# Two stacked pairs of a memory attention and a hedgehog linear attention on one core: fewer VectorE operations in layer A's features, another chain for layer B's query sums, and a new order

## The chip, the cores and the metric

The kernel runs on 1 core of one Trainium2 chip. The metric is the device time of that core in microseconds (us), from the start to the end of one execution; lower is better.

## The reference, cut to what matters

The input x is 2048 tokens by 512 in bf16. Two kinds of layers, each with 32 heads of 16, are applied twice in the order A, B, A, B, always on the normalized input and with a residual.

```python
# layer A: four segments of 512 tokens, memory M, z carried from one to the next
q, k, v = x @ wq, x @ wk, x @ wv
phi = lambda t: where(t > 0, t + 1.0, exp(t))
for s in range(4):
    a_dot = softmax(qs @ ks.T * 0.25 + causal mask) @ vs
    a_mem = (phi(qs) @ M) / (phi(qs) @ z + 1e-6)
    o = g * a_mem + (1 - g) * a_dot          # g = sigmoid(beta), one per head
    M, z = M + phi(ks).T @ vs, z + phi(ks).sum()
x = x + concat(o) @ wo
# layer B: no mask
pq, pk = q @ w_phi, k @ w_phi
phi_q = [softmax(pq), softmax(-pq)]          # phi_k likewise
kv, z = phi_k.T @ v, phi_k.sum()
x = x + (phi_q @ kv) / (phi_q @ z + 1e-6) @ wo
```

## The kernel before, in words

The kernel holds x in SBUF as 16 tiles of 128 tokens (`X`) and runs the four layers as one program. It is first written down as a list of operations (`Graph.op`), each with its engine, the tiles that it reads and the tiles that it opens. Then a table that is stored in the kernel as a packed text, `ORDER`, says for every operation its place in the one global order, for some of them the engine (an evacuation out of PSUM made by `evac` may go to ScalarE, L359, or to VectorE, L360), and for every tile its buffer. `place` reads the table and `emit` derives the semaphore waits from it. So the order on each engine is that of the table, and an edit that adds or removes an operation comes with a new table.

All of PSUM is four buffers of 128 x 1024 f32 (the pool `D` in the names of the profile). Projections, scores, numerators, sums and transposes each take one of the four. In SBUF the names are those of pools: `p` for general tiles, `pX` for the transposed inputs, `pQ` and `pK` for the masked keys and the queries of layer A, `pV` and `pW` for values, `pF` and `pE` for exponentials, `pT` for weighted values of layer B, `pS` for small sums.

**Normalizing a tile** (`ln`): VectorE makes the statistics (L584, L585); the reciprocal root is an Ln and an Exp on ScalarE (L588, L590) for the four tiles of the first segment and two GpSimd operations (L592, L594) for the others; VectorE normalizes (L605). The result is transposed by DMA or, for the tiles listed in `PE_T`, by TensorE: `tpe` (L379) does eight matmuls with an identity into a PSUM buffer of f32, and an evacuation of 512 columns writes them to bf16.

**Layer A** (`a_proj`, `a_att`): keys, queries and values by matmuls in pairs of row halves (`pair`, L341); the features phi (`phi`, L634) as an exponential on ScalarE (L351) and on VectorE a maximum with 0 (L642), a minimum of the exponential with 1 (L643) and the sum of both (L644); key copies masked by row groups (`kmask`, L651 or L653); scores by matmuls (L326), their exponentials on ScalarE (L351), the products with the values (L326), and on VectorE the reciprocal of the sums, the product (L878) and the addition of the memory's part (L882). `out_proj` multiplies by wo and adds the residual on VectorE (L933).

**Layer B, keys** (`b_keys`, `kv_add`): exponentials of both signs, their sums per head (L980), the values times the reciprocal sums (L1016 straight from PSUM; L1008 from a copy, for pairs listed in `VCOP`), and KV accumulated over all tokens (L946), masked into `Rkv` and `Rz` (L950, L953). Where a residual of layer B is listed in `RES_PE`, the pair of tiles gets X by four matmuls with the identity into its PSUM buffer and ScalarE copies the sum to X (L359).

**Layer B, queries** (`b_query`), four chunks of 512 tokens in each pair of layers. The projection and its two exponentials per group come first. Then 128 small matmuls (L326, from `Rz`) put four sums per head and token into one PSUM buffer `ZQ`: for each sign the softmax's own sum and the sum against z. The weights of both signs are worked out of them by Ln and Exp of -1 on ScalarE (L351, 128 columns each, twice) and by VectorE (L1069 to L1080). Chunk 0 does this from PSUM; chunks 1 to 3 (`ZCOP`) first copy the sums to SBUF and so free the buffer. After that, tile by tile: 16 small matmuls from `Rkv` make the numerators N, a ScalarE copy takes them to SBUF (for tiles in `COPIED`), VectorE multiplies by the weights (L1099 from the copy, L1102 from PSUM), adds both signs (L1105), and transposing and `out_proj` follow. In the first pair of layers the queries and layer A of the second pair run interleaved; in the last pair the queries stand alone at the end, and every two tiles (the last two singly, `SOLO`) are stored when their residual is done.

At the start TensorE does warm-up matmuls on a constant (`warm`, L666) until the first transposed tiles are there.

Of the kernel before, what the change touches and what calls it, by code (L numbers as in the profile page):

```python
# [10 lines left out]
ALU = mybir.AluOpType  # L11
# [286 lines left out]
class Kernel:  # L298
# [72 lines left out]
    def tpe(self, out_ap, src, reads, writes, opens=(), label="", ev=None):  # L371

        ps = self.T(self.pD, "gen")

        def fn(e):
            for k in range(4):
                for hf in range(2):
                    r = slice(64 * hf, 64 * hf + 64)
                    ins = e.matmul(ps.t[:, hf * 512 + k * 64:hf * 512 + k * 64 + 64], src()[r, k * 128:(k + 1) * 128], self.ident[r, r], start=True, stop=True,  # L379
                                   tile_position=(64 * hf, 0))  # L380
            return ins
        self.g.op({"pe": (112.0, fn)}, list(reads) + [self.R("ident")], [ps], opens=opens, label=label + "p", rows=64)
        halves = lambda: ps.t[:].rearrange("p (h x) -> p h x", h=2)[:, :, 0:256].rearrange("p h (a c) -> p h a c", a=4)
        if ev:
            self.evac(ev[0], lambda: ev[1](halves()), 512, [ps], writes, label=label + "e")
        else:
            self.evac(lambda: out_ap().rearrange("p a (h c) -> p h a c", h=2), halves, 512, [ps], writes, label=label + "e")
# [11 lines left out]
    def alloc(self):  # L399
# [10 lines left out]
        self.tri = sb("tri", [128, 64], BF16)  # L410
        self.ones8 = sb("ones8", [128, 8], F32)
# [41 lines left out]
    def setup(self):  # L453
# [66 lines left out]
        for hf in range(2):  # L520
            v(lambda e, hf=hf: e.tensor_copy(self.tri[64 * hf:64 * hf + 64, :], tw.t[64 * hf:64 * hf + 64, 64 * hf:64 * hf + 64]), 100,
              [tw], [R("tri", hf)])
        v(lambda e: e.memset(self.epsln[:], LN_EPS), 70, [], [R("epsln")])
# [57 lines left out]
    def ln(self, t, xT, flex=False, pe=False, root="pool"):  # L581
        R, v = self.R, self.v
        tt = t % 4
        v(lambda e: e.bn_stats(self.stats[:, t, :], self.X[:, t, :]), 602, [R("X", t)], [R("st", t)], label="bn")  # L584
# [29 lines left out]

    def wproj(self, ps, Ws, wres, gs, xT, opens=(), label=""):
# [20 lines left out]
    def phi(self, dst, src, e_, keys, c0, n):  # L636
# [5 lines left out]
        v(lambda e: e.tensor_scalar(cut(dst), cut(src), 0.0, None, op0=ALU.max), 68 + n / 3.84, S, D, label="phmax", port=True)  # L642
        v(lambda e: e.tensor_scalar(cut(e_), cut(e_), 1.0, None, op0=ALU.min), 68 + n / 3.84, E, E, label="phmin", port=True)  # L643
        v(lambda e: e.tensor_tensor(cut(dst), cut(dst), cut(e_), ALU.add), 68 + n / 1.92, D + E, D, label="phadd", port=True)  # L644
# [154 lines left out]
    def a_att(self, L, s, i0):  # L799
# [11 lines left out]
        for gg in range(2):  # L811
            PV = self.T(self.pD, "pv")
            for g in (2 * gg, 2 * gg + 1):
# [5 lines left out]
                for j in range(i0 + 1):  # L819
# [18 lines left out]
                self.mm(lambda S=S, key=key, qry=qry: [  # L838
                    (S.t[:, hf * 512 + p * 192 + 64 * (1 - x):hf * 512 + p * 192 + 192 - 128 * x], key(hf, i0 + 1, p, x), qry(hf, 128 + 64 * x, 128 - 64 * x), p + x == 0, False)
                    for p in range(2) for x in range(2) for hf in range(2)] + [  # L840
                    (S.t[:, hf * 512:hf * 512 + 384].rearrange("p (a b) -> p a b", a=2)[:, :, 0:128], two(hf), tri(hf, 4), False, True) for hf in range(2)],
                    [], rd + trir, [S], opens=[PE], label="Sd", rows=64, dur=286)
                self.act(lambda PE=PE: PE.t[:, :, 64:256], lambda S=S: S.t[:, :].rearrange("p (a b) -> p a b", a=2)[:, :, 0:384].rearrange("p a (c e) -> p a c e", c=2),
                         ACT.Exp, 768, [S], [PE], scale=0.25, label="expd")

# [184 lines left out]
    def b_query(self, L, c, store):  # L1030
# [13 lines left out]
        zv = lambda s, k: ZQ.t[:, :].rearrange("p (a x) -> p a x", a=2)[:, :, 0:256].rearrange("p a (s k x) -> p a s k x", s=2, k=2)[:, :, s, k, :]  # L1044
# [8 lines left out]
        inps = (L, c) not in ZCOP  # L1053
        if not inps:
            ZS = self.T(self.p2, "T")
            two = lambda x: x.rearrange("p (a x) -> p a x", a=2)
            self.evac(lambda: two(ZS.t[:].bitcast(F32)), lambda ZQ=ZQ: two(ZQ.t[:])[:, :, 0:256], 512, zr, [ZS], label="Zev")
            zr = [ZS]
            zv = lambda s, k: two(ZS.t[:].bitcast(F32)).rearrange("p a (s k x) -> p a s k x", s=2, k=2)[:, :, s, k, :]
# [224 lines left out]
```

## Time and profile before

| | before |
|---|---|
| times of 3 runs, us | 468.32, 468.88, 470.64 (median 468.88) |
| profiled execution: its own time | 468.75 |
| its span in the trace | 466.7 |
| mean granted TensorE clock | 0.992 |
| busy: PE (TensorE) | 446.3 |
| busy: ACT (ScalarE) | 423.3 |
| busy: DVE (VectorE) | 420.2 |
| busy: POOL (GpSimd) | 56.2 |

The times are those of the whole execution on the device; the span runs from the first to the last instruction in the trace of one profiled execution. Busy time is the time in which at least one instruction of the engine ran. Matmuls overlap, so a busy TensorE need not be at its peak. In rows of groups the columns are line, engine, operation, output and input with shapes, count, then busy time and the mean in ns of one, then the idle time ahead of them and what ended it. In rows of the timeline they are the start, the length, and then the instructions. In rows of stretches of the span they are the bounds and the length, the busy times of PE, PEld (weight loads), DVE, ACT and POOL with the number of instructions, the granted clock, the DMA share and GB/s.

### The profile page before, as it was taken

To read this page: it belongs to the slowest core of one execution; us is meant where nothing else is said; L and a number is where in the kernel's file an instruction comes from. 1 tells how busy PE (TensorE), PEld (TensorE's weight loads), DVE (VectorE), ACT (ScalarE), POOL (GpSimd) and SP (SyncE) were. 2 spreads that over 40 slices of the span, in tenths; PEclk is the share of its full clock that TensorE was granted. 3 is DMA by queue.
4 is the path that set the end of the run, shared out by engine and by line. 5 is a ranking of instruction groups with operands and counts; after the bars stand their busy time and mean duration, and the time that the engine had idled before them with its cause. 6 is when DMAs were issued, how large, how long until landed. Compare 5 with 4: busy or idle time off the path is not lost.

```text
span 466.7 us, 25467 instructions
## 1 busy us (share of the span) xinstructions
PE 446.3 (96%) x11789; PEld 298.7 (64%) x11789; DVE 420.2 (90%) x800; ACT 423.3 (91%) x552; POOL 56.2 (12%) x138
## 2 busy tenths in 40 slices
PE   8999999999999999998999999999999999999987
PEld 4557756666666776665556776666677677666553
DVE  5999999798799978989999999999997897998985
ACT  3899999999999997689999999999999999677892
POOL 1411123001101101100331022020110020110000
PEclk9999999999999999999999999999999999999799
DMA  8943363631254131100254435344133214200255
GB/s 247 229 107 85 49 82 57 93 55 25 50 75 63 29 47 27 31 3 14 37 83 58 61 73 82 60 70 62 25 50 62 38 26 51 36 13 3 55 86 171
DMA packets 87756, 29.97 MB, mean 64 GB/s; under 512 B 74322, under 2 KB 87650, under 8 KB 87650
## 3 DMA queue, kind: packets, MB, share of 16 engines
q1 hardware_dynamic: 86818, 27.81, 34.4%
q8 instruction: 92, 1.51, 1.4%
q10 hardware_dynamic: 800, 0.52, 0.4%
q14 instruction: 14, 0.11, 0.1%
q0 software_dynamic: 32, 0.02, 0.0%
HBM read 6.31 MB, written 2.10 MB: 18 GB/s over the span
## 4 chain that ended last, share of the span: by engine, by line
PE 57%; ACT 34%; DVE 4%; DMA 3%; issue 2%; POOL 1%; SPq 0%; DVEq 0%
PE D L341 36%; PE D L326 18%; ACT p L351 18%; ACT pF L351 9%; ACT pE L351 4%; DMA p<-p 2%; PE D L666 2%; DMA pX<-p 1%; ACT pS L351 1%; DVE X L933 1%; ACT p L359 1%; DVE p L795 1%; DVE pK L360 0%; POOL rstd L594 0%; ACT X L359 0%
## 5 line engine op out<-in xcount | busy, mean ns | idle before, releaser
L351 ACT ACTIVATE p<-D 128x1024 bf16<-128x1024 f32 (+1 forms) x224 | 221.0, 1027 | 14.5 <-PE D L341 10.2
L326 PE MATMUL D<-pK,pQ 64*128 64x256 bf16 (+3 forms) x1536 | 114.2, 243 | 5.1 <-ACT p L351 1.3
L351 ACT ACTIVATE pF<-D 128x896 bf16<-128x896 f32 x128 | 116.5, 940 | 1.5 <-PE D L326 1.0
L326 PEld LDWEIGHTS D<-pK,pQ 64*128 64x128 bf16 x1536 | 55.4, 94 | 41.5 <-ACT pF L351 5.6
L326 PE MATMUL D<-pV,pF 64*128 64x34 bf16 x1024 | 76.4, 175 | 1.4 <-ACT pF L351 0.8
L326 PE MATMUL D<-pW,pF 64*128 64x34 bf16 x1024 | 73.3, 175 | 0.0
L326 PEld LDWEIGHTS D<-pV,pF 64*128 64x128 bf16 x1024 | 57.0, 93 | 4.1 <-ACT pF L351 1.7
L592 POOL TENSOR_SCALAR rstd<-mv 128x1 f32<-128x1 f32 x60 | 16.2, 275 | 351.8 <-DVE mv L585 351.7
L326 PE MATMUL D<-pV,p 64*128 64x34 bf16 x1024 | 53.9, 176 | 0.2 <-DVE MS L755 0.2
L351 ACT ACTIVATE pE<-D 128x768 bf16<-128x768 f32 x64 | 52.1, 823 | 2.1 <-PE D L326 1.9
L326 PEld LDWEIGHTS D<-pW,pF 64*128 64x128 bf16 x1024 | 52.9, 93 | 0.9
L326 PE MATMUL D<-pW,p 64*128 64x34 bf16 x1024 | 52.7, 176 | 0.0
L326 PEld LDWEIGHTS D<-pV,p 64*128 64x128 bf16 x1024 | 47.9, 93 | 3.4 <-DVE MS L755 0.4
L326 PEld LDWEIGHTS D<-pW,p 64*128 64x128 bf16 x1024 | 46.4, 93 | 2.2
L326 PE MATMUL D<-tri,two 64*128 64x128 bf16 (+1 forms) x384 | 46.7, 234 | 0.0
L584 DVE BATCH_NORM_STATS2 stats<-X 128x6 f32<-128x512 bf16 x64 | 42.6, 681 | 3.8 <-DMA X<-in_A_x_dram 3.6
L326 PE MATMUL D<-pV,pE 64*128 64x34 bf16 x512 | 45.3, 175 | 0.5 <-issue 0.5
L326 PE MATMUL D<-pW,pE 64*128 64x34 bf16 x512 | 42.9, 175 | 0.0
L980 DVE TENSOR_REDUCE pS<-p 128x64 f32<-128x1024 bf16 (+1 forms) x36 | 38.6, 1090 | 0.3 <-ACT p L351 0.2
L594 POOL TENSOR_TENSOR rstd<-rstd,mhalf 128x1 f32<-128x1 f32 x60 | 37.9, 639 | 2.4
L933 DVE TENSOR_TENSOR X<-X,D 128x1024 bf16<-128x1024 bf16 (+1 forms) x30 | 32.1, 1074 | 6.4 <-PE D L341 6.2
L341 PE MATMUL D<-pX,WA_q 64*128 64x512 bf16 x256 | 37.1, 376 | 0.5 <-issue 0.4
(133 smaller groups left out, 998.5 us busy)
## 6 DMA issues: line engine op xcount, KB each, us to landing
pW<-pV SPq DMA_DIRECT2D x16, 136.0 KB, 2.8
out_dram<-X SPq DMA_DIRECT2D x7, 256.0 KB, 2.3
X<-in_A_x_dram SPq DMA_DIRECT2D x3, 512.0 KB, 7.5
pX<-in_B_wqkv_dram SPq DMA_DIRECT2D x3, 512.0 KB, 4.6
p<-p SPq DMA_TRANSPOSE x73, 3.1
pX<-p SPq DMA_TRANSPOSE x54, 3.2
WA_k<-in_A_wk_dram SPq DMA_DIRECT2D x2, 256.0 KB, 6.5
WA_v<-in_A_wv_dram SPq DMA_DIRECT2D x1, 512.0 KB, 7.1
```

What stands on the lines that cost most here:

```text
L326: ins = e.matmul(out_ap, lhsT, rhs, start=st, stop=sp, tile_position=(basep(lhsT), basep(out_ap)))
L341: ins = e.matmul(out_ap, lhsT[64 * hf:64 * hf + 64], rhs[64 * hf:64 * hf + 64], start=k == 0 and i == 0, stop=k == 1 and i == len(lists[hf ...
L351: return self.g.op({"act": (dur, lambda e: e.activation(out_ap(), in_ap(), func, scale=scale))}, reads, writes, opens, label=label)
L359: ch = {"act": (n / 1.2 + 51, lambda e: e.activation(out_ap(), in_ap(), ACT.Copy)), "dve": ((340 if fast else n / 0.96 + 65), lambda e: e. ...
L584: v(lambda e: e.bn_stats(self.stats[:, t, :], self.X[:, t, :]), 602, [R("X", t)], [R("st", t)], label="bn")
L592: v(lambda e: e.tensor_scalar(rs, self.mv[:, t, 1:2], LN_EPS, None, op0=ALU.add), 170, [R("mv", t)], [R("rstd", t)], eng="pool", label="rstd")
L594: v(lambda e: e.tensor_tensor(rs, rs, self.mhalf[:], ALU.pow), 540, [R("rstd", t), R("mhalf")], [R("rstd", t)], eng="pool", label="rstd")
L666: ins = e.matmul(D.t[c0:, r0 * 8:r0 * 8 + n], r[:, c0:], ones(r, n), start=True, stop=True, tile_position=(r0, c0))
L795: v(lambda e: e.tensor_tensor(tmp.t[:].rearrange("p (y h r d) -> p y h r d", y=16, h=2, r=2), NM.t[:, :].rearrange("p (h y r d) -> p y h r ...
L933: self.v(lambda e: e.tensor_tensor(X(), X(), src(), ALU.add), 65 + 512 * n / 0.96, pr + xr, xr, label="res")
L980: fn = lambda e, sgn=sgn, eo=eo, Z=Z, n=n: e.tensor_reduce(Z.t[:, 0:64 * n].rearrange("p (k s h) -> p k s h", k=n, s=2)[:, :, sgn, :], eo( ...
```

## The change

It has seven parts.

1. **phi** in two VectorE operations: max(x, 0) + 1 in one, then the minimum of that and the exponential; the operation L643 is dropped.
2. **`tpe`** writes its transposes as bf16 into PSUM (`is_transpose`), and its evacuation reads bf16.
3. **Query sums**: Ln and Exp of -1 over both signs in one call of 256 columns, straight from PSUM in all chunks; one product (L1085) makes the ratios of both signs, a second operation (L1086) adds them with 1e-6, then Ln and Exp of 128 columns and one product (L1090). The copies of the sums (`ZCOP`) are gone.
4. **The first segment's tile 3** (`LN_ACT`) is normalized with statistics made on ScalarE by accumulating activations (`ln_act`); only its last operation stays on VectorE.
5. **Residuals**: `RES_PE` is empty, so all are added on VectorE (L958 after the change); the 24 identity matmuls and six ScalarE copies are gone.
6. **Copies**: all numerators go through ScalarE's copy (`COPIED`), and one value pair of each last key stage is copied first (`VCOP`). A mask `keep` is made once; the branch that would use it (`TRI_E`) is empty.
7. **`ORDER`** is new.

```diff
 def tpe
-  ins = e.matmul(ps.t[:, hf * 512 + k * 64:hf * 512 + k * 64 + 64], ..., start=True, stop=True, ...)
+  ins = e.matmul(pb()[:, hf * 1024 + k * 64:hf * 1024 + k * 64 + 64], ..., start=True, stop=True, is_transpose=True, ...)
...
 def ln_act
+  a(680, lambda e: e.activation(xn.t[:], self.X[:, t, :], ACT.Copy, accum_out=st(0)), ...)
+  a(100, lambda e: e.activation(st(1), st(0), ACT.Copy, scale=-1.0 / D), ...)
+  a(780, lambda e: e.activation(xn.t[:], self.X[:, t, :], ACT.Square, bias=st(1), accum_out=st(2)), ...)
+  a(185, lambda e: e.activation(st(3), st(2), ACT.Ln, scale=1.0 / D, bias=self.epsln[:, 0:1]), ...)
+  a(100, lambda e: e.activation(st(3), st(3), ACT.Exp, scale=-0.5), ...)
+  self.v(lambda e: e.tensor_scalar(xn.t[:], self.X[:, t, :], st(1), st(3), op0=ALU.add, op1=ALU.mult), 300, ...)
...
 def phi
-  v(lambda e: e.tensor_scalar(cut(dst), cut(src), 0.0, None, op0=ALU.max), ...)
-  v(lambda e: e.tensor_scalar(cut(e_), cut(e_), 1.0, None, op0=ALU.min), ...)
-  v(lambda e: e.tensor_tensor(cut(dst), cut(dst), cut(e_), ALU.add), ...)
+  v(lambda e: e.tensor_scalar(cut(dst), cut(src), 0.0, 1.0, op0=ALU.max, op1=ALU.add), ...)
+  v(lambda e: e.tensor_tensor(cut(dst), cut(dst), cut(e_), ALU.min), ...)
...
 def b_query
-  if not inps:
-      self.evac(lambda: two(ZS.t[:].bitcast(F32)), lambda ZQ=ZQ: two(ZQ.t[:])[:, :, 0:256], 512, zr, [ZS], label="Zev")
...
-  self.act(lambda: u(0), lambda: zv(1, 1), ACT.Ln, 128, zr, [t1[0]], psum=inps, label="zln")
-  self.act(lambda: u(0), lambda: u(0), ACT.Exp, 128, [t1[0]], [t1[0]], scale=-1.0, psum=False, label="zln")
-  v(lambda e: e.tensor_tensor(u(0), u(0), zv(0, 1), ALU.mult), ...)
...
+  self.act(wide, lambda: zv(1), ACT.Ln, 256, zr, [t1], label="zlA")
+  self.act(lambda: t1.t[:], lambda: t1.t[:], ACT.Exp, 256, [t1], [t1], scale=-1.0, psum=False, label="zlA")
+  v(lambda e: e.tensor_tensor(y(), wide(), zv(0), ALU.mult), ...)
+  v(lambda e: e.scalar_tensor_tensor(ys(1), ys(0), 1e-6, ys(1), op0=ALU.add, op1=ALU.add), ...)
+  self.act(lambda: ys(1), lambda: ys(1), ACT.Ln, 128, [AB[1]], [AB[1]], psum=False, label="zlB")
+  self.act(lambda: ys(1), lambda: ys(1), ACT.Exp, 128, [AB[1]], [AB[1]], scale=-1.0, psum=False, label="zlB")
+  v(lambda e: e.tensor_tensor(..., split(t1.t[:]), ys(1)..., ALU.mult), ...)
...
-ZCOP = {(L, c) for L in range(2) for c in (1, 2, 3)}
-VCOP = set()
+TRI_E = set()
+LN_ACT = 3
+VCOP = {(0, 3), (1, 3)}
...
-RES_PE = {(0, t) for t in (2, 3, 6, 7)} | {(1, t) for t in (2, 3, 6, 7, 8, 9, 10, 11)}
+RES_PE = set()
```

Lines shift: L351, L359, L360, L341 and L326 stay where they are, the others move by 1 to 25 (L605 becomes L610, L878 becomes L903, L933 becomes L958, L1016 becomes L1041, L1099 becomes L1111, L1105 becomes L1117, L666 becomes L686, L379 becomes L380).

What moves is shown at three places. The first is the start of the program. On ScalarE before, from its first computation to the first evacuation of a transposed tile (`rstd` is a tile's reciprocal root, `gt` the gate of layer A, `D` a PSUM buffer):

```order
L588 ACTIVATE rstd<-mv,epsln 128x1 x2
L590 ACTIVATE rstd<-rstd 128x1
L588 ACTIVATE rstd<-mv,epsln 128x1
L590 ACTIVATE rstd<-rstd 128x1 x2
L588 ACTIVATE rstd<-mv,epsln 128x1
L351 ACTIVATE gt<-D 128x32
L590 ACTIVATE rstd<-rstd 128x1
L359 ACTIVATE pX<-D 128x2x4x64 x3
```

After, at the same place:

```order
L626 ACTIVATE p,stats<-X 128x512
L627 ACTIVATE stats<-stats 128x1
L628 ACTIVATE p,stats<-X,stats 128x512
L593 ACTIVATE rstd<-mv,epsln 128x1
L629 ACTIVATE stats<-stats,epsln 128x1
L595 ACTIVATE rstd<-rstd 128x1
L593 ACTIVATE rstd<-mv,epsln 128x1
L630 ACTIVATE stats<-stats 128x1
L593 ACTIVATE rstd<-mv,epsln 128x1
L595 ACTIVATE rstd<-rstd 128x1
L351 ACTIVATE gt<-D 128x32
L595 ACTIVATE rstd<-rstd 128x1
```

Tile 3's two passes of 512 columns stand ahead of all roots now, its root stands among them, and the gate's exponential still stands ahead of the last root. On TensorE before, from the gate's matmul on (`onesb` marks the warm-up, `ident` the transposes of the normalized tiles; buffers are numbered here):

```order
L326 MATMUL D1<-beta_sb,onesb 128x32
L666 MATMUL D0<-onesb 128x512 x4
L379 MATMUL D2<-ident,p11 128x64 x8
L666 MATMUL D0<-onesb 128x512 x2
L379 MATMUL D3<-ident,p12 128x64 x8
```

After, at the same place:

```order
L326 MATMUL D1<-beta_sb,onesb 128x32
L686 MATMUL D0<-onesb 128x512 x8
L380 MATMUL D2<-ident,p12 128x64 x8
L686 MATMUL D0<-onesb 128x512 x2
L380 MATMUL D3<-ident,p11 128x64 x8
```

Eight warm-up matmuls instead of four stand between the gate's matmul and the first transposes. The second place is the queries of the last pair of layers. On TensorE before, from the last projections ahead of the first query sums (`pX,WB_q` is a query projection, `Rz` the sums, `Rkv` the numerators):

```order
L341 MATMUL D<-pX,WB_q 128x512 x16
L326 MATMUL D<-Rz,p 128x2x4 x112
L326 MATMUL D<-Rkv,p 128x64 x16
L326 MATMUL D<-Rz,p 128x2x4 x16
L326 MATMUL D<-Rkv,p 128x64 x32
L326 MATMUL D<-Rz,p 128x2x4 x32
L326 MATMUL D<-Rkv,p 128x64 x16
L326 MATMUL D<-Rz,p 128x2x4 x32
L326 MATMUL D<-Rkv,p 128x64 x32
L341 MATMUL D<-pX,WB_q 128x512 x16
```

After, at the same place:

```order
L341 MATMUL D<-pX,WB_q 128x512 x8
L326 MATMUL D<-Rz,p 128x2x4 x112
L326 MATMUL D<-Rkv,p 128x64 x16
L326 MATMUL D<-Rz,p 128x2x4 x16
L341 MATMUL D<-pX,WB_q 128x512 x8
L326 MATMUL D<-Rkv,p 128x64 x32
L326 MATMUL D<-Rz,p 128x2x4 x48
L326 MATMUL D<-Rkv,p 128x64 x16
L326 MATMUL D<-Rz,p 128x2x4 x16
L341 MATMUL D<-pX,WB_q 128x512 x8
L326 MATMUL D<-Rkv,p 128x64 x48
```

Two groups of query projections stand between the small matmuls now, where before all of them stood ahead of or behind them. The third place is VectorE beside this, from the last mask of `Rkv` on; before:

```order
L950 TENSOR_TENSOR Rkv<-KV,H 128x512 x2
L1069 TENSOR_TENSOR pS<-pS,D 128x128
L1071 TENSOR_TENSOR pS<-pS,D 128x128
L1072 TENSOR_TENSOR pS<-pS,D 128x128
L1073 SCALAR_TENSOR_TENSOR pS<-D,pS 128x128
L360 COPY p<-D 128x512
L1080 TENSOR_TENSOR pS<-pS 128x8x16
L1102 TENSOR_TENSOR p<-D,pS 128x1024
L1105 TENSOR_TENSOR p<-p 128x512
```

After:

```order
L975 TENSOR_TENSOR Rkv<-KV,H 128x512 x2
L1085 TENSOR_TENSOR pS<-pS,D 128x2x2x64
L1086 SCALAR_TENSOR_TENSOR pS<-pS 128x128
L1090 TENSOR_TENSOR pS<-pS 128x4x4x16
L1085 TENSOR_TENSOR pS<-pS,D 128x2x2x64
L1111 TENSOR_TENSOR p<-p,pS 128x1024
L1086 SCALAR_TENSOR_TENSOR pS<-pS 128x128
L1117 TENSOR_TENSOR p<-p 128x512
```

The second chunk's sums were copied out (L360) ahead of the first chunk's weights; now its first product (L1085) reads PSUM, between the first chunk's weights and its first product with N.

More of the change, by code (lines that the diff above doesn't have):

```diff
@@ L373, in tpe @@
         ps = self.T(self.pD, "gen")
+        pb = lambda: ps.t[:, :].bitcast(BF16)
         def fn(e):
@@ L583, in ln @@
         tt = t % 4
+        if root == "all":
+            return self.ln_act(t, xT)
         v(lambda e: e.bn_stats(self.stats[:, t, :], self.X[:, t, :]), 602, [R("X", t)], [R("st", t)], label="bn")
@@ L1122, in lnA @@
             for t in range(s * 4, s * 4 + 4):
-                self.ln(t, self.xA[(L, s)], pe=("xA", L, t) in PE_T, root="act" if L == 0 and s == 0 else "pool")
+                self.ln(t, self.xA[(L, s)], pe=("xA", L, t) in PE_T, root=("all" if t == LN_ACT else "act") if L == 0 and s == 0 else "pool")
         for L in range(2):
```

193 lines of the change are left out of this document (100 added, 93 removed).

## The prediction

> **What bounds the kernel now.** I read the page's first parts first: busy time by engine, the granted clock by slices, and the shares of the chain that ended last.
>
> ```profile
> PE 446.3 (96%) x11789; PEld 298.7 (64%) x11789; DVE 420.2 (90%) x800; ACT 423.3 (91%) x552; POOL 56.2 (12%) x138
> PEclk9999999999999999999999999999999999999799
> PE 57%; ACT 34%; DVE 4%; DMA 3%; issue 2%; POOL 1%; SPq 0%; DVEq 0%
> ```
>
> Three engines are nearly full, and two of them, TensorE and ScalarE, make 91% of the chain. VectorE is as busy as ScalarE but ends a wait for only 4% of the span (18.7 us). So an instruction taken from VectorE is worth little by itself, and one taken from ScalarE or TensorE is worth something only in the stage that this engine bounds. I therefore cut the span where the work changes: layer A of the first pair, the start of the first layer B queries, the middle, the last key stage, and the last queries.
>
> ```profile
> 24.00:180.00 156.00, 150.32 (x4434) 105.24 (x4428) 141.94 (x261) 153.10 (x187) 17.59 (x41) 1.00 0.38 62
> 206.00:216.00 10.00, 8.42 (x322) 5.78 (x320) 7.81 (x19) 9.48 (x16) 0.00 (x0) 1.00 0.01 3
> 216.00:394.00 178.00, 173.10 (x4800) 118.08 (x4796) 165.04 (x312) 174.47 (x217) 25.58 (x56) 1.00 0.36 55
> 394.00:428.00 34.00, 33.94 (x680) 22.52 (x676) 31.49 (x52) 25.29 (x37) 3.07 (x8) 1.00 0.14 22
> 428.00:466.70 38.70, 32.23 (x792) 19.30 (x792) 29.83 (x59) 27.54 (x44) 0.00 (x0) 0.90 0.43 94
> ```
>
> The columns are length, then busy time on PE, weight loads, VectorE, ScalarE, GpSimd, then the clock. ScalarE bounds 24 to 180 (153.10 of 156) and 206 to 394 (174.47 of 178 in the second part), with TensorE close behind (173.10 of 178). From 394 to 428 TensorE alone bounds (33.94 of 34, ScalarE 25.29). From 428 on nobody is full and the mean clock is 0.90: here the time goes into chains.
>
> The sum is made against the profiled execution: span 466.7 us in a run of 468.75, so 2.05 us lie around the span. The median of the runs shown, 468.88, is 0.13 above that run.
>
> **ScalarE and TensorE work that goes or comes.**
>
> ```profile
> L341 PE MATMUL D<-X,ident 64*128 64x512 bf16 x24 | 4.6, 378 | 0.2 <-ACT X L359 0.2
> L359 ACT ACTIVATE X<-D 128x1024 bf16<-128x1024 f32 x6 | 6.2, 1036 | 4.4 <-PE D L341 4.4
> L359 ACT ACTIVATE p<-D 128x512 f32<-128x512 f32 x3 | 1.8, 599 | 0.0
> L351 ACT ACTIVATE pS<-pS 128x128 f32<-128x128 f32 x28 | 9.0, 322 | 4.4 <-DVE pS L980 3.8 <-DVE pS L1073 0.4
> L351 ACT ACTIVATE p<-D 128x1024 bf16<-128x1024 f32 x216 | 216.3, 1043 | 12.1 <-PE D L341 7.8 <-PE D L326 3.5
> L933 DVE TENSOR_TENSOR X<-X,D 128x1024 bf16<-128x1024 bf16 x22 | 26.8, 1217 | 5.2 <-PE D L341 4.9
> ```
>
> Six residual pairs lose four identity matmuls each. ScalarE loses six copies into X, three copies of query sums, and gains four copies of N (L1099's source) at 1.04. Its Ln and Exp on query sums become 256 wide in two of four calls per chunk; no row shows that width, so it lies between 322 ns (128) and 1043 ns (1024). By a straight line, 0.80 ns an element, it is 0.42 us: 16 calls by 0.1 are 1.6 us, half in each pair of layers.
>
> Between 206 and 394, where ScalarE bounds, two residual copies (2.1) and one sum copy (0.6) go and 0.8 comes: 1.9 us; overlap of neighbours eats little of it. **Term 1: -1.9.** The ends are 0, if TensorE, 4.9 us short of full there, keeps the stretch, and -5.4, if ScalarE's 3.5 us of idle closes too. The eight identity matmuls of this stage lie under ScalarE's exponentials and count nothing; without that cover they are 8 x 0.19 = 1.5 us at most.
>
> From 428 on ScalarE loses four residual copies (4.1) and two sum copies (1.2), gains four N copies (4.2) and 0.8 of width, and one exponential of the queries (1.0) stands ahead of the first sums now: -1.3. TensorE loses 16 identity matmuls, 3.1 us by the row's busy share. The chain there passes from ScalarE to TensorE, so I take ScalarE's sum, the nearer one. **Term 2: -1.3**, ends +1.0 and -3.1.
>
> At the very end the residuals were shared between two engines:
>
> ```profile
> 462.54 1.02 ACT L359 ACTIVATE X<-D 128x1024 bf16<-128x1024 f32 x1 [4.42 <-PE D L341]
> 463.66 0.69 DVE L933 TENSOR_TENSOR X<-X,D 128x512 bf16<-128x512 bf16 x1 [0.97 <-PE D L341]
> ```
>
> Now VectorE does both in series. The last matmuls of the pair would end near 462.5, the sum takes 1.22, and the last tile's 0.69 follows: 464.4 at the earliest in place of 464.35, more if VectorE comes late from the tiles ahead, whose pairs take 1.22 against 1.74 us of matmuls. **Term 3: +0.4**, ends 0 and +1.5.
>
> **VectorE.**
>
> ```profile
> L643 DVE TENSOR_SCALAR p<-p 128x1024 bf16<-128x1024 bf16 x22 | 9.1, 413 | 0.0
> L360 DVE CAST p<-D 128x512 bf16<-128x512 f32 x11 | 7.5, 679 | 1.5 <-PE D L901 1.5
> L651 DVE TENSOR_SCALAR pQ<-p,m 128x512 bf16<-128x512 bf16 x15 | 4.7, 341 | 0.3 <-ACT p L359 0.3
> L360 DVE COPY p<-D 128x512 f32<-128x512 f32 x3 | 2.1, 692 | 1.0 <-PE D L326 0.9
> L1075 DVE SCALAR_TENSOR_TENSOR pS<-p 128x128 f32<-128x128 f32 x6 | 1.7, 283 | 0.0
> L757 DVE TENSOR_TENSOR MSb<-MS,GAm 128x272 bf16<-128x272 f32 x12 | 5.1, 428 | 0.0
> L1102 DVE TENSOR_TENSOR p<-D,pS 128x1024 bf16<-128x1024 f32 x4 | 4.9, 1221 | 0.1
> L1099 DVE TENSOR_TENSOR p<-p,pS 128x1024 bf16<-128x1024 bf16 x28 | 18.7, 685 | 2.0 <-ACT p L351 1.7
> L1016 DVE TENSOR_TENSOR pT<-D,pT 128x1024 bf16<-128x1024 f32 x28 | 33.0, 1213 | 1.0 <-PE D L341 0.9
> L1008 DVE TENSOR_TENSOR pT<-p,pT 128x512 bf16<-128x512 bf16 x8 | 2.9, 396 | 0.0
> ```
>
> The minimum of layer A's features (22 x 0.413 and four halves) saves 10.2. Ten copies of 512 out of f32 PSUM become six out of bf16 PSUM; that copy has no row and lies between 0.341 (all bf16, in SBUF) and 0.679 (f32 PSUM). I take 0.45, nearer the first because the type is the same: 6.8 becomes 2.7. Three sum copies go (2.1). Forty operations of 0.28 on query sums become eight of 0.28 and 16 of twice the width at 0.43: -2.1. Four N products leave PSUM (4 x 0.54 = 2.1). The two value pairs at the ends of the key stages become one more copy of 1.22 and eight products of 0.396 for four of 1.213: -0.5. Against this stand six residual pairs, 7.3. With the tile that ScalarE normalizes (0.9) the sum is -14.7 of 420.2, or -13.4 with the slow copy. It lies beside exponentials and matmuls; scaled to the 18.7 us of VectorE on the chain it is 14.7 / 420.2 x 18.7. **Term 4: -0.6**, ends 0 and -6.4, all the ScalarE idle of the two long stretches (2.9 and 3.5), for VectorE is the engine that hands ScalarE its PSUM buffers and operands.
>
> **The first tile.**
>
> ```profile
> 7.89 0.61 PE L666 MATMUL D<-onesb 64*128 64x512 bf16 x4
> 8.32 0.30 PE L379 MATMUL D<-ident,p 64*128 64x64 bf16 x8
> 8.67 1.67 ACT L359 ACTIVATE pX<-D 128x512 bf16<-128x512 f32 x3 [0.28 <-PE D L379]
> 10.66 0.37 PE L341 MATMUL D<-pX,WA_k 64*128 64x512 bf16 x1 [0.31 <-ACT pX L359]
> ```
>
> The first projection waits for three evacuations on ScalarE, and those for the first transposes. VectorE saves one tile's statistics (0.85), but the gate's exponential, which waits for TensorE, still stands ahead of the last root on ScalarE. Ahead of the first transposes stand eight warm-up matmuls in place of four, 0.43 us more. **Term 5: +0.4**, ends -0.4 (the statistics count after all) and +0.8.
>
> **The clock.** In these rows TensorE's clock falls, in the queries of the last pair:
>
> ```profile
> 429.00:430.00 1.00, 0.86 (x66) 0.77 (x62) 1.00 (x2) 0.95 (x2) 0.00 (x0) 1.00 0.00 0
> 432.00:433.00 1.00, 0.63 (x26) 0.47 (x20) 0.97 (x3) 0.53 (x2) 0.00 (x0) 0.50 0.00 0
> 438.00:439.00 1.00, 0.93 (x10) 0.34 (x10) 1.00 (x3) 0.82 (x5) 0.00 (x0) 0.76 0.33 71
> 428.91 0.95 PE L326 MATMUL D<-Rz,p 64*128 64x8 bf16 x64
> 436.26 3.10 PE L341 MATMUL D<-pX,WB_q 64*128 64x512 bf16 x16
> 210.85 1.02 PE L341 MATMUL D<-pX,WB_q 64*128 64x512 bf16 x8
> 215.40 1.04 PE L341 MATMUL D<-pX,WB_q 64*128 64x512 bf16 x8
> ```
>
> From 428.91 to 436.26 only matmuls of 8 and 64 columns run; three microseconds into that the clock is 0.50. At the same point of the first pair the query projections stand between the small ones, never over 3.7 us apart, and the clock stays 1.00. The change's order puts such projections between the small ones here too. I take it that the drop goes: the sixteen projections at 436.26 take 3.10 instead of two times about 0.9, and the small ones of this time a little over half a microsecond more than their like at 216. **Term 6: -1.9**, ends 0 (drop stays) and -3.0. [...]
>
> Sum: -1.9 - 1.3 + 0.4 - 0.6 + 0.4 - 1.9 = -4.9, and 468.75 - 4.9 = 463.9 us.
>
> **Rivals.**
>
> *Cover.* In 206 to 394 TensorE takes over when ScalarE gets lighter, VectorE's relief stays under it, and the clock falls again, since sums still wait for a chain of four ScalarE operations with nothing wide behind. Then terms 1, 4 and 6 vanish: 468.75 - 1.3 + 0.8 = 468.2. For it speak the 4.9 us by which TensorE is short of full; against it the projections' new place.
>
> *The held buffer, slower.* All of PSUM is four buffers. Before, chunks 1 to 3 copied their sums out (0.60 or 0.69) and freed the buffer. Now the buffer is held through Ln, Exp and the first product, 0.42 + 0.42 + 0.43, and through whatever each engine does between, one ScalarE copy of 1.04 and one VectorE product of 0.685: 3.0, or 2.3 longer, six times, 13.8 us. If half of it reaches TensorE, whose next matmuls need that buffer, and terms 1 and 6 fail with it, the time is 468.75 - 1.5 + 6.9 = 474. It decides when the wait for a query-sum buffer goes beyond about 0.8 us a chunk (4.9 over six). Against it: in the first chunk, which never copied, TensorE was 8.42 of 10 busy, and the buffer held there cost under 1.6.
>
> *Relief counts.* VectorE's 14.7 us let ScalarE's idle close in both stretches: term 4 is -6.4 and the time 458.
>
> [...]
>
> **How the numbers follow.** This kernel's measurement tells about 0.5% (2.3 us) from no change, so faster means under 466.5 and slower over 471.2. My sum, 461 to 466.4, has 0.44; transposes 0.04 (465.8); relief 0.14 (455.5 to 461); cover 0.25 (466.5 to 471); the held buffer 0.13 (471.3 to 477). Faster is 0.44 + 0.04 + 0.14 = 0.62, same 0.25, slower 0.13. The range leaves out the held buffer and the lower part of relief: 456.5 to 471.
>
> **What would show it.** Right: no slice under 1.00 after 420; ScalarE still full from 24 to 180; VectorE near 406 busy, its bf16 PSUM copies near 0.45; the first projection near 11.1; the last key stage unchanged in length; under 0.5 us of waits of TensorE for the query sums' products. Wrong: a stretch of 0.50 in the last queries (term 6), TensorE idle before query sums until VectorE's first product (the held buffer), a last residual that starts over 1 us after the last matmul (term 3), or long waits for VectorE in 394 to 428.

## The result, and the profile after

The changed kernel takes 472.37 us (median of 22 runs, 469.67 to 475.68) against 469.63 us for the kernel before (22 runs, 468.32 to 471.05): ratio 1.006, 95% interval 1.0043 to 1.0076. It is slower by 0.6%; I had forecast 463.9. The profiled execution after took 472.04 us with a span of 470.0; before it was 468.75 and 466.7.

The page's first parts after the change: busy time by engine, the granted clock, the shares of the chain.

```profile
PE 443.2 (94%) x11765; PEld 295.0 (63%) x11765; DVE 410.4 (87%) x761; ACT 426.9 (91%) x556; POOL 56.0 (12%) x139
PEclk9989999999999999999999999999999999999999
PE 61%; ACT 22%; DVE 13%; issue 2%; DMA 1%; POOL 1%; DVEq 0%
```

The clock is full after 420, as forecast, but a slice near 29 us is below, and VectorE has 13% of the chain in place of 4%. The stages of the prediction, after the change:

```profile
24.00:180.00 156.00, 145.81 (x4258) 101.74 (x4256) 133.62 (x239) 147.43 (x180) 17.44 (x40) 0.99 0.33 55
216.00:394.00 178.00, 171.53 (x4798) 115.49 (x4794) 162.21 (x297) 174.69 (x218) 25.36 (x56) 1.00 0.35 54
428.00:470.00 42.00, 34.12 (x872) 20.67 (x868) 35.01 (x65) 31.36 (x47) 0.00 (x0) 0.99 0.39 87
```

From 24 to 180 ScalarE has 147.43 where it had 153.10: nearly six microseconds of its idle time are new, in the stretch for which I had expected it to stay full.

Fixed times mix stages once one is late, so I compare one event: the masking of KV (`Rkv`), which ends layer B's keys in each pair of layers. Before:

```profile
206.41 1.28 DVE L950 TENSOR_TENSOR Rkv<-KV,H 128x512 bf16<-128x512 f32 x2
428.76 1.29 DVE L950 TENSOR_TENSOR Rkv<-KV,H 128x512 bf16<-128x512 f32 x2
```

After:

```profile
212.64 1.28 DVE L975 TENSOR_TENSOR Rkv<-KV,H 128x512 bf16<-128x512 f32 x2
434.62 1.28 DVE L975 TENSOR_TENSOR Rkv<-KV,H 128x512 bf16<-128x512 f32 x2
```

Up to the first mask the change loses 6.23 us, between the masks it gains 0.37, and from the second to the end of the span (37.94 before, 35.38 after) 2.6. The whole loss lies ahead of the first mask. TensorE's timeline after the change shows its place:

```profile
24.48 0.38 PE L326 MATMUL D<-pK,pQ 64*128 64x256 bf16 x4
29.39 1.89 PE L341 MATMUL D<-pX,WA_k 64*128 64x512 bf16 x8 [4.54 <-DMA pX<-p]
31.05 0.66 PE L326 MATMUL D<-pK,pQ 64*128 64x256 bf16 x4
31.48 1.54 PE L341 MATMUL D<-pX,WA_k 64*128 64x512 bf16 x8
32.85 0.39 PE L326 MATMUL D<-pK,pQ 64*128 64x256 bf16 x4
33.06 1.04 PE L341 MATMUL D<-pX,WA_q 64*128 64x512 bf16 x8
```

TensorE stands 4.54 us before the second segment's first projection, for a DMA, and the next eight matmuls take 1.89 where eight of the same shape take 1.04 at 33.06. The granted clock in stretches of 2 us there:

```profile
26.00:28.00 2.00, 0.00 (x0) 0.00 (x0) 1.52 (x8) 0.83 (x1) 1.29 (x4) 1.00 0.81 150
28.00:30.00 2.00, 0.61 (x4) 0.34 (x6) 0.00 (x0) 0.00 (x0) 1.19 (x3) 0.77 0.74 158
30.00:32.00 2.00, 2.00 (x15) 0.90 (x12) 0.00 (x0) 0.25 (x1) 0.00 (x0) 0.50 0.66 135
```

So the stall is paid twice, as idle time and as half clock behind it. The DMA is a transpose of the normalized second segment. SP's queue, from which it is issued, before and after:

```profile
14.78 1.29 SPq L364 DMA_TRANSPOSE pX<-p  x1
16.12 0.57 SPq L460 DMA_DIRECT2D pX<-in_B_wqkv_dram  x1
16.73 5.04 SPq L364 DMA_TRANSPOSE pX<-p  x3
```

```profile
15.26 0.59 SPq L462 DMA_DIRECT2D pX<-in_B_wqkv_dram  x1
15.89 1.15 SPq L462 DMA_DIRECT2D WA_o<-in_A_wo_dram  x2
17.09 0.43 SPq L462 DMA_DIRECT2D pX<-in_B_wqkv_dram  x1
17.56 3.03 SPq L364 DMA_TRANSPOSE pX<-p  x1
20.64 0.58 SPq L462 DMA_DIRECT2D WB_o<-in_B_wo_dram  x1
21.27 6.42 SPq L364 DMA_TRANSPOSE pX<-p  x3
```

The new order issues all three 512 KB loads of layer B's projections, all of layer A's output weights and seven of the eight 64 KB loads of layer B's output weights ahead of the first transpose. What the four transposes then take from issue to landing (minimum, median, maximum), before and after:

```profile
DMA to landing us min/median/max: 2.7/4.0/5.6
```

```profile
DMA to landing us min/median/max: 2.7/6.4/10.0
```

The last is issued at 26.4 in place of 20.2, though VectorE has normalized the last of the four tiles by 20.44, against 19.89 before. The last of the three 512 KB loads lands at 26.89, and the transposes behind it at 27.57 to 29.15. The first transpose, issued at 17.56 behind all three, lands 10.0 us later, 0.68 us behind the last of them.

### The profile page after: what moved, and what is told of

It reads as the page before. It is cut to its first block, busy times and chain, and to the rows that moved or that the text cites. A ratio compares the mean times of both kernels' runs of the same rounds, so it can differ in the third digit from the quotient of the medians.

```text
span 470.0 us, 25380 instructions
## 1 busy us (share of the span) xinstructions
PE 443.2 (94%) x11765; PEld 295.0 (63%) x11765; DVE 410.4 (87%) x761; ACT 426.9 (91%) x556; POOL 56.0 (12%) x139
## 4 chain that ended last, share of the span: by engine, by line
PE 61%; ACT 22%; DVE 13%; issue 2%; DMA 1%; POOL 1%; DVEq 0%
PE D L341 37%; PE D L326 22%; ACT p L351 11%; ACT pF L351 6%; ACT pE L351 3%; DVE p L1111 2%; PE D L686 2%; DVE X L958 2%; DVE stats L589 2%; DVE pQ L671 1%; DVE p L610 1%; ACT pS L351 1%; DMA p<-p 1%; DVE p L1117 1%; DVE pV L360 1%
## 5 line engine op out<-in xcount | busy, mean ns | idle before, releaser
L351 ACT ACTIVATE p<-D 128x1024 bf16<-128x1024 f32 (+1 forms) x228 | 226.1, 1023 | 16.3 <-PE D L341 8.0
L326 PE MATMUL D<-pK,pQ 64*128 64x256 bf16 (+3 forms) x1536 | 115.1, 244 | 5.1 <-ACT pE L351 0.9
L351 ACT ACTIVATE pF<-D 128x896 bf16<-128x896 f32 x128 | 116.1, 936 | 1.9 <-PE D L326 1.3
L326 PEld LDWEIGHTS D<-pK,pQ 64*128 64x128 bf16 x1536 | 54.7, 94 | 43.1 <-ACT pF L351 5.7
L326 PE MATMUL D<-pV,pF 64*128 64x34 bf16 x1024 | 76.0, 176 | 0.5 <-ACT pE L351 0.2
L326 PE MATMUL D<-pW,pF 64*128 64x34 bf16 x1024 | 73.5, 176 | 0.0
L326 PEld LDWEIGHTS D<-pV,pF 64*128 64x128 bf16 x1024 | 56.7, 93 | 4.2 <-issue 1.3
L351 ACT ACTIVATE pE<-D 128x768 bf16<-128x768 f32 x64 | 52.7, 828 | 2.4 <-PE D L326 2.0
L326 PEld LDWEIGHTS D<-pW,pF 64*128 64x128 bf16 x1024 | 53.4, 93 | 1.3
L326 PE MATMUL D<-pV,p 64*128 64x34 bf16 x1024 | 53.2, 176 | 0.1
L326 PE MATMUL D<-pW,p 64*128 64x34 bf16 x1024 | 52.1, 176 | 0.6 <-issue 0.6
L326 PEld LDWEIGHTS D<-pV,p 64*128 64x128 bf16 x1024 | 47.4, 93 | 3.7 <-issue 1.1
L326 PEld LDWEIGHTS D<-pW,p 64*128 64x128 bf16 x1024 | 46.1, 93 | 2.6 <-issue 0.8
L326 PE MATMUL D<-tri,two 64*128 64x128 bf16 (+1 forms) x384 | 46.3, 234 | 0.0
L326 PE MATMUL D<-pV,pE 64*128 64x34 bf16 x512 | 45.1, 175 | 0.0
L341 PE MATMUL D<-pX,WA_k 64*128 64x512 bf16 x256 | 38.7, 389 | 5.4 <-DMA pX<-p 4.5
L958 DVE TENSOR_TENSOR X<-X,D 128x1024 bf16<-128x1024 bf16 (+1 forms) x36 | 39.3, 1097 | 4.7 <-PE D L341 4.3
L326 PE MATMUL D<-pW,pE 64*128 64x34 bf16 x512 | 43.1, 175 | 0.0
L341 PE MATMUL D<-pX,WA_q 64*128 64x512 bf16 x256 | 37.1, 377 | 0.7 <-DVE p L610 0.6
```

Of the source, the lines that this page charges most:

```text
L326: ins = e.matmul(out_ap, lhsT, rhs, start=st, stop=sp, tile_position=(basep(lhsT), basep(out_ap)))
L341: ins = e.matmul(out_ap, lhsT[64 * hf:64 * hf + 64], rhs[64 * hf:64 * hf + 64], start=k == 0 and i == 0, stop=k == 1 and i == len(lists[hf ...
L351: return self.g.op({"act": (dur, lambda e: e.activation(out_ap(), in_ap(), func, scale=scale))}, reads, writes, opens, label=label)
L958: self.v(lambda e: e.tensor_tensor(X(), X(), src(), ALU.add), 65 + 512 * n / 0.96, pr + xr, xr, label="res")
```

## The experiments

Theory: SP's queue is the cause of the loss, and what I had summed is right beside it. Rivals: the tiles are normalized late, or later parts of the change cost as well. The first four kernels move loads and nothing else; the list of loads is that of `setup`, 15, 16 and 18 the 512 KB ones of layer B, 19 to 26 its output weights, 10 to 13 layer A's output weights, a quarter each (e4 moves all four, e6 and e10 two of them). Each ratio is to the kernel before as it ran beside the experiment on the same chip: 471.87 us for e1 to e4, 470.9 for e6 to e9, 470.67 for e10 and e11, 471.22 for e12 and e13.

**e1**, in `place`, on the changed kernel (`foldT` are the transposes of layer B's weights, `xnT` those of the inputs, `otr` those of the attention outputs, `vsw` the swaps of the values' halves):

```diff
+loads = [o for o in self.ops if o.label == "load"]
+late, last = [loads[i] for i in (15, 16, 18)], [loads[i] for i in range(19, 27)]
+order = [o for o in order if o not in late + last]
+at = lambda label, k: order.index([o for o in order if o.label == label and o.kind == "d"][k])
+k = at("foldT", 7) + 1
+order[k:k] = last
+k = at("xnT", 3) + 1
+order[k:k] = late
```

> The kernel after with eleven weight loads of layer B (three of 512 KB, eight of 64 KB) moved behind the four transposes of the second segment in SP's queue; nothing else changes. Theory (queue): the 4.54 us of idle of TensorE at 24.86 and the 3.41 us at half clock behind it (1.7 us lost) go; 472.4 - 6.2 = 466.2 us, and the last masked KV of the first pair comes 5 to 7 us earlier than in the kernel after. Rival (late operands): the transposes are late because VectorE and GpSimd normalize these tiles later; then the gap stays and the time is 471 to 473. Rival (later buffers): the head is only a part, and the time comes back to 469 to 470.

Measured: 478.28 us, ratio 1.0145 (1.0115 to 1.0176). Slower still. The two waits of TensorE for DMAs from 20 to 70:

```profile
PE D L349 <- DMA p<-p: 6.7, 1, 6.7
PE D L334 <- DMA pW<-pV: 1.5, 1, 1.5
```

The wait for the inputs is gone, so the transposes were not late for their tiles; but the moved loads stand in front of other transfers now, the value swaps (1.5) and the transposes for layer A (6.7, with 10.24 us at half clock from 58.88 on). The first mask comes at 217.41, later than with the change. My expected time was wrong, since I had looked only at what the loads stood in front of and not at what they would stand in front of.

**e2** moves only the output weights, **e3** only the three large loads, by the same lines with one of the two lists empty.

> The kernel after with only the eight 64 KB loads of layer B's output weights moved behind. They are 0.5 MB, eight of the eleven issues, about 0.6 us of SP each. Theory of bytes in the queue: at some 300 GB/s they are worth 1.7 us of the last landing, so the gap of 4.54 shrinks to about 2.9 and the time is 469.5 to 471. Rival (issuing time): eight issues of 0.6 are 4.8 us of SP ahead of the transposes, so the gap goes nearly whole and the time is 466 to 467.5.

Measured: 474.81 us, ratio 1.0057 (1.0038 to 1.0075).

> The kernel after with only the three 512 KB loads of layer B's projection weights moved behind. They are 1.5 MB in three issues, 1.6 us of SP. Theory of bytes: 5 us of the last landing, so the gap of 4.54 goes and the time is 466 to 467.5. Rival (issuing time): 1.6 us of the gap go, and the time is 470 to 471.

Measured: 474.58 us, ratio 1.0052 (1.0027 to 1.0078). In e2 TensorE still waits 3.1 us for the inputs, near the 2.9 of bytes in the queue (that is at 300 GB/s; in the change's profile the DMAs move 283 on average from 8 to 24); in e3 not at all. So bytes count there and issuing time little. Both times come from new waits as in e1 (2.7 us for `p<-p` in e2; 2.3 and 2.3 for `pW<-pV` and `p<-p` in e3) and tell nothing more; the first masks, at 215.05 and 214.31, are later than with the change too.

**e4** is the converse, on the kernel before:

```diff
+early = [loads[i] for i in (15, 18, 10, 11, 12, 13, 19, 20, 21, 22, 23, 24, 25, 26)]
+order = [o for o in order if o not in early]
+k = order.index([o for o in order if o.label == "xnT" and o.kind == "d"][0])
+order[k:k] = early
```

> The kernel before, with two of the 512 KB loads, the eight 64 KB loads of layer B's output weights and four halves of layer A's output weights put ahead of the first transpose of the second segment (a third 512 KB load cannot move, since its buffer is still in use). Theory (queue): the fourth transpose lands 2 to 4 us later than 23.4, TensorE stands idle before the second segment's first projection by 1 to 3 us, and the time rises by 1 to 4 us over the kernel before (471 to 474). Rivals by which the order of loads is harmless: within 1 us of the kernel before.

Measured: 478.05 us, ratio 1.0133 (1.0097 to 1.0169), more than the 1 to 4 us that I had expected. The old kernel stalls at the new one's place, and its first mask of KV comes at 214.74, 8.33 late:

```profile
PE D L346 <- DMA pX<-p: 4.9, 1, 4.9
```

The way there is another one. The loads moved ahead keep SP issuing until 22.6, and the transposes, issued then, land 2.5 us after their issue, where the change's took up to 10.0:

```profile
16.48 6.12 SPq L465 DMA_DIRECT2D WB_o<-in_B_wo_dram  x8
22.65 5.23 SPq L369 DMA_TRANSPOSE pX<-p  x4
```

```profile
DMA to landing us min/median/max: 2.5/2.5/2.6
```

So here SP's issuing time counts, and in e2 and e3 the bytes. Either way the order of loads alone is enough for more than the change lost.

**e6** spreads the loads of the changed kernel by need:

```diff
+wbo, late, wao = loads[19:27], [loads[16], loads[15]], [loads[11], loads[12]]
+order = [o for o in order if o not in wbo + late + wao]
+for k, o in enumerate(wbo):
+    order.insert(900 + 40 * k, o)
+k = at("foldT", 5) + 1
+order[k:k] = wao
+k = at("vsw", 1) + 1
+order[k:k] = late
```

> The kernel after with the loads spread by need: one 512 KB load ahead of the second segment's transposes, the other two behind the value swaps that follow them, half of layer A's output weights behind the sixth transpose of weights, the eight 64 KB loads of layer B's output weights one by one far later (about 90 us on). Theory (queue): the transposes land near 24, none of the two gaps of the runs so far (4.5 or 3.1 at 25, 2.7 or 6.7 at 57) is left, TensorE stays at full clock at the start, and the last masked KV of the first pair comes 5 to 7 us earlier than in the kernel after: 6.2 us under the kernel after, that is 2.5 to 4 us under the kernel before (ratio 0.991 to 0.995). Rival (the rest of the change costs as well): the gaps go, and the time is still at or over the kernel before (ratio 0.999 or more).

Measured: 469.94 us (before 470.9 on this chip), ratio 0.9983 (0.9959 to 1.0007). That is 0.77% less than the change's 1.006, and lies between what the theory (0.991 to 0.995) and the rival (0.999 or more) gave. The wait at 25 is gone, but the profiled execution waits 3.0 us for `p<-p` and runs at half clock from 57.16 to 63.98; its first mask, at 212.00, comes 0.64 us earlier than with the change and not 5 to 7.

**e7** to **e9** undo or load one part each on top of e6.

```diff
-v(lambda e: e.tensor_scalar(cut(dst), cut(src), 0.0, 1.0, op0=ALU.max, op1=ALU.add), ...)
+quarter = lambda t, k: t.t[:, c0 + k * n // 4:c0 + (k + 1) * n // 4]
+v(lambda e: [e.tensor_scalar(quarter(dst, k), quarter(src, k), 0.0, 1.0, op0=ALU.max, op1=ALU.add) for k in range(4)][3], ...)
```

> The kernel of the spread loads, with VectorE's maximum in layer A's features made in four quarters in place of one piece, so that VectorE is busy some 10 us more, about what the dropped minimum cost. The result is the same. Theory (VectorE's time is covered): within 1 us of the spread loads. The prediction's share, 10 / 420 of VectorE's 18.7 us on the chain: +0.4 us. Rival (relief counts): +3 us or more.

Measured: 471.41 us, ratio 1.0015 (0.9988 to 1.0043), 1.5 us over e6 with intervals that overlap. VectorE's busy time grew by 4.5 us (414.8 against 410.3), not by 10; why is not shown. The time does not tell the prediction's +0.4 from +3: undecided.

```diff
-RES_PE = set()
+RES_PE = {(0, t) for t in (2, 3, 6, 7)} | {(1, t) for t in (2, 3, 6, 7, 8, 9, 10, 11)}
```

> The kernel of the spread loads, with part 5 undone: six residual pairs by identity matmuls on TensorE and a copy on ScalarE again, 24 matmuls and six copies more, six VectorE sums of 1.22 us fewer. The prediction's terms: 1.9 us of the first pair's stretch that ScalarE bounds, and some 1.3 us at the end, come back: +1.5 to +3 us over the spread loads. Theory of cover: nothing in the first pair, +0.5 to +1.5 at the end. Rival (VectorE's sums at the end cost more than they save): faster than the spread loads by 0.5 or more.

Measured: 477.1 us, ratio 1.0137 (1.0095 to 1.0178), 7.2 over e6. (The copies of the sums are also fixed to ScalarE.) The sign is that of the prediction, the size more than twice it. The copies stand on ScalarE where VectorE's sums stood in an order made for VectorE, so this prices the old residuals in the new order, not by themselves.

```diff
-ins = e.matmul(pb()[:, hf * 1024 + k * 64:hf * 1024 + k * 64 + 64], ..., is_transpose=True, ...)
+ins = e.matmul(ps.t[:, hf * 512 + k * 64:hf * 512 + k * 64 + 64], ...)
```

> The kernel of the spread loads, with part 2 undone: TensorE's transposes go to f32 PSUM and the copies read f32. VectorE's copies take 0.68 us again. Theory: within 0.7 us of the spread loads, since there are six such copies on VectorE. Rival (the transposing mode does not hold up the clock): the spread loads show a stretch of 0.50 in the last queries or the first tiles, which goes here, and this kernel is faster by 1 us or more.

Measured: 470.81 us, ratio 0.9986 (0.9961 to 1.0012), like e6. Both profiles have the same two stretches of half clock, near 57 and 221, so the transposing mode is not their cause here.

**e10** goes on from e6:

```diff
+swap = [o for o in order if o.label == "xnT" and o.kind == "d"][4]
...
+order.insert(at("otr", 1) + 1, swap)
-k = at("foldT", 5) + 1
+k = at("foldT", 3) + 1
```

> The kernel of the spread loads with two more moves in SP's queue: half of layer A's output weights behind the fourth transpose of weights, where SP stood idle, in place of behind the sixth, and one transpose of the third segment's input behind the transpose of the first attention output, for which TensorE waited 3.05 us at 55.4. Theory (SP's queue is what remains of the head): that wait shrinks under 1 us and the half clock behind it goes, 3 to 5 us less in the profiled execution; on average, since the executions of the spread loads differ by their stretches at half clock, 1 to 3 us less (ratio to the kernel before 0.992 to 0.996). Rival (another wait takes its place): the ratio stays at 0.998.

Measured: 469.21 us (before 470.67), ratio 0.9973 (0.9944 to 1.0002). Its median is the lowest of all versions of the change, 1.5 us under the kernel before, though the interval just takes in no change and e6 is not told from it; the ratio lies between my forecast (0.992 to 0.996) and the rival (0.998). The wait at 55.4 that it was to shrink is gone. The masks of KV in its trace:

```profile
208.64 1.28 DVE L987 TENSOR_TENSOR Rkv<-KV,H 128x512 bf16<-128x512 f32 x2
431.84 1.29 DVE L987 TENSOR_TENSOR Rkv<-KV,H 128x512 bf16<-128x512 f32 x2
```

The first comes 4.0 us earlier than after the change and is still 2.23 late; of its waits from 24 to 60 the profile lays 2.6 us to issue and none to a DMA. Executions differ here: e11 and e12, the same program up to this mask, have it at 207.84 and 209.36, and e13, the kernel before up to it, at 207.13. So on average about 2 us of the head are left (208.6 against 206.8), and their cause is open.

**e11** and **e12** add two pairs and one pair of wide matmuls on a constant behind every 16 small ones of the first two chunks' query sums, on top of e10; **e13** adds the one pair to the kernel before.

```diff
+[(ZQ.t[:, hf * 512 + 256:hf * 512 + 512]..., self.onesb[64 * hf:64 * hf + 64, :],
+  self.onesb[64 * hf:64 * hf + 64, None, :].to_broadcast([64, 2, 128]), True, True) for hf in range(2) if c < 2]
```

> The kernel with the two moves, and two pairs of matmuls of 256 columns on a constant behind every 16 small matmuls for the query sums of chunks 0 and 1, into columns of the same PSUM buffer that nothing reads: 1.7 us of TensorE more in each pair of layers. Theory (the half clock follows stretches of small matmuls): no stretch of 0.50 in the queries, near 220 or after 420, in the profiled execution; the mean granted clock of all executions is 0.995 or more, and their spread shrinks; the time is within 1.5 us of the kernel with the moves, since the matmuls cost what the clock gives. Rival (the half clock has another cause): stretches of 0.50 at the same places and 1 to 3.5 us more time.

> The kernel with the two moves in SP's queue, and one pair of matmuls of 256 columns on a constant (half of those before) behind every 16 small matmuls for the query sums of chunks 0 and 1: 0.9 us of TensorE more in each pair of layers. Theory (the half clock follows the stretches of small matmuls, and a little is enough): the mean clock is 0.995 or more in nearly all executions and the time 0 to 1.5 us under the kernel with the moves (ratio to the kernel before 0.994 to 0.998). Rival (the fillers lie on the path of the first query sums, at 2.3 us for 0.9 us of matmuls as the full ones did): ratio 1.000 to 1.004.

> The kernel before with the same light fillers and nothing else. Theory of term 6 (its half clock at 431.8 to 438.6 follows the small matmuls of the first query sums): that stretch is gone or halved in the profiled execution, the mean clock of the executions rises from 0.988 to 0.993 to 0.995 or more; the time is 0 to 2 us less than the kernel before, as far as the fillers' 1.8 us leave it (ratio 0.996 to 1.000). Rival (the clock falls there for another reason): the stretch stays, and the time is 1 to 4 us more.

Measured: e11 473.75 us, ratio 1.0060 (1.0035 to 1.0085); e12 471.71 us, ratio 1.0003 (0.9979 to 1.0027); e13 475.57 us, ratio 1.0090 (1.0061 to 1.0119). The clock by slices of the profiled executions, of e10, e12 and e13:

```profile
PEclk9999999999999999998999999999999999999999
```

```profile
PEclk9999999999999999999999999999999999999999
```

```profile
PEclk9999999999999999998999999999999999999799
```

The granted clock over the 12 executions is on average 0.9942 in e10, 0.9976 in e12 and 0.9981 in e11: on the new order the clock is higher with the fillers, as expected (e11's profile keeps one stretch, near 437), and they cost more than they give: 4.5 us in e11's median against e10, where I had expected at most 1.5, and e12 comes out at its rival's ratio. On the kernel before they lift nothing (0.9892, before itself 0.9910) and cost 4 us. So it is not shown that the half clock of the first queries follows the small matmuls, and what would prevent it stays open.

## Why the prediction was wrong

**The step that failed is the head of the sum.** For the time ahead of the first mask of KV it has nothing of its own but term 5, "The first tile": "Ahead of the first transposes stand eight warm-up matmuls in place of four, 0.43 us more. Term 5: +0.4, ends -0.4 [...] and +0.8." For the first tile nothing speaks against it (first projection at 11.01, forecast near 11.1), though e10 to e12, with one and the same head, have that projection at 10.54 to 11.47. But I took the head to be that tile, held ScalarE to be full from 24 to 180, and did not count the loads that the new order moves on SP's queue ahead of the second segment's transposes; no term and no rival held them. Of the 6.23 us lost by the first mask of KV, 4.54 are idle time of TensorE there, and up to 1.7 more the matmuls lose in 3.41 us at half clock. e1, e3, e6 and e10 take that wait away and e4 makes one at the same place in the old kernel, so the cause of the wait is shown: the order of the loads. That nothing else costs in the head is not shown: in e10, without the wait and the half clock, 4.0 of the 6.23 us come back. (I put it down to the new waits behind the moved loads that the times of the four differ.)

**Terms 1 and 4** (-1.9 and -0.6): between the masks only 0.37 us came, which is within what executions differ by (e3, with the same order there and the clock full, takes 223.16 us where the change took 221.98 and the kernel before 222.35). ScalarE is as full as before from 216 to 394 (174.69), so the copies taken from it did not shorten the stretch; the rival "cover" described this part. VectorE's busy time fell by 9.8 us, not 14.7; its durations add up to 15.6 less, but I had summed durations, and busy time counts instructions that overlap once. ScalarE got busier, 426.9 after 423.3: the four evacuations of transposed tiles that I took off VectorE ("Ten copies [...] become six") went to it at 0.60 us each, and I had put them into no term; tile 3's statistics came on top. The durations that I had bounded came out near:

```profile
L360 DVE COPY p<-D 128x512 bf16<-128x512 bf16 x4 | 1.6, 408 | 0.0
L351 ACT ACTIVATE pS<-D 128x256 f32<-128x256 f32 x8 | 3.1, 394 | 0.0
L1085 DVE TENSOR_TENSOR pS<-pS,D 128x256 f32<-128x256 f32 x8 | 3.3, 417 | 4.2 <-ACT pS L351 4.2
```

The copy out of bf16 PSUM takes 0.408 (I took 0.45), Ln over 256 columns 0.394 (0.42), the first product 0.417 (0.43). Their prices were right, and still brought little in a stretch that was bound elsewhere.

**Terms 2, 3 and 6** (-1.3, +0.4, -1.9, together -2.8): from the second mask to the end 2.6 us were gained in the profiled executions. The sum fits, and its parts do not. Term 3 by itself: the last sums after the change,

```profile
465.72 1.82 DVE L958 TENSOR_TENSOR X<-X,D 128x1024 bf16<-128x1024 bf16 x2 [0.74 <-PE D L341]
```

end at 467.54, 0.75 us behind TensorE's last matmuls (464.64 and 2.15), so nothing was lost there, where I had 0.4. Term 6 came true in the profile of the change by luck. e3 has the change's order in the last queries, and there the clock falls as in the kernel before, three microseconds behind the second mask:

```profile
437.47 1.29 DVE L983 TENSOR_TENSOR Rkv<-KV,H 128x512 bf16<-128x512 f32 x2
440.40:443.81 3.41, 2.61 (x110) 2.17 (x108) 2.53 (x8) 3.41 (x8) 0.00 (x0) 0.50 0.02 5
443.81:447.23 3.42, 3.24 (x74) 1.96 (x68) 3.31 (x8) 3.07 (x8) 0.00 (x0) 0.50 0.40 77
```

So the projections between the small matmuls do not hold the clock up by themselves. And from that mask to the end of its span (473.4) e3 takes 35.9 us, 0.5 more than the change at full clock (e1, e2, e6 and e10, at full clock there too, take 35.3 to 35.5) and 2.0 less than the kernel before: term 6 is worth about 0.5 and not 1.9, and the other parts of the change gained some 2.0 at the end, more than terms 2 and 3 together (-0.9). How these 2.0 divide among them is open. Over all executions the clock did not rise: 0.9906 on average in 22 of the changed kernel, 0.9907 in the 18 of the kernel before beside e1 to e4. With the head mended it is higher, 0.9942 against 0.9905 in e10.

**The held buffer** decided nothing. TensorE does wait there, in the last queries:

```profile
PE D L326 <- DVE pS L1085: 1.9, 2, 1.1
```

1.9 us in two waits, not 6.9 over six: the mechanism is there, and I had set its price too high. (Beside it I wrote -1.5 for the rest of the sum; without terms 1 and 6 it is -1.1.)

**The 0.04 for "transposes" (465.8)** has no run behind it: no run shows that transposing matmuls fail to hold up the clock. What the runs show is e9, with the old transposes, at 470.81 us where e6 took 469.94, and half clock near 57 and 221 in both.

Taken together, -0.4 and -2.6 beside the head make -3.0 us, where I had summed -5.3 without term 5. With the head mended as far as e10 goes, -1.5 us are left.

## What to carry to other kernels

When an order changes, read every queue in it, first those that compute nothing: ask of each DMA what stands in front of it now, in bytes and in time to issue, and when its reader comes for it. A load that is needed at 60 us or 200 us costs nothing late and much when a transpose needed at 25 us stands behind it (here 4.54 us of TensorE); but moving it back only helps if nothing urgent stands behind its new place. And a wait of TensorE of several microseconds is to be priced with the half clock that can follow it (3.41 us behind the change's 4.54, 10.24 behind e1's 6.7, none behind e2's 3.1).

## What was not expected of the hardware

- The clock falls in portions: 3.41 us at half clock behind the stall, 6.83 in the old kernel's last queries, 10.24 in e1 behind the wait of 6.7. Not each wait brings one: behind e2's wait of 3.1 us near 25 and e3's of 2.3 near 30 the clock stays full. How much of the span it is down changes from execution to execution of one program: over 23 executions of the kernel before beside e10 the mean clock lay between 0.985 and 0.996.
- TensorE need not be idle for it. In the 3.4 us ahead of the fall, in the kernel before and in e10, and TensorE's work in the first of these:

```profile
428.24:431.65 3.41, 2.73 (x144) 2.02 (x142) 2.70 (x8) 2.75 (x5) 0.00 (x0) 1.00 0.03 5
```

```profile
213.70:217.10 3.40, 1.78 (x84) 1.33 (x80) 3.32 (x8) 3.40 (x5) 0.00 (x0) 1.00 0.02 5
```

```profile
L326 PE MATMUL D<-Rz,p 64*128 64x8 bf16 x120 | 2.0, 163 | 0.7 <-ACT p L351 0.7
L341 PE MATMUL D<-pX,WB_q 64*128 64x512 bf16 x8 | 1.0, 378 | 0.1
```

  TensorE was busy for 2.73 and 1.78 us, and in the kernel before 2.0 of that were matmuls of 8 columns. That these count for little for the clock is a guess of mine: the mean clocks with fillers in e11 and e12 (0.9981 and 0.9976, 0.9942 in e10) fit it, that of e13 (0.9892, 0.9910 without them) does not bear it out, so it is not shown.
